# Attention and feed-forward outputs through DRAM as one float32 array, split where they are loaded

## The chip, the cores and the metric

The kernel runs on one core of one Trainium2 chip. The metric is the device time of one execution in microseconds (us); the median of three runs of the kernel before is 1112.55 us. A core has five engines with a queue of instructions each: PE (TensorE, matrix products), DVE (VectorE), ACT (ScalarE), POOL (GpSimd) and SP (SyncE, which issues every DMA of this kernel).

## The reference

Causal attention with a forget gate over 4 batches x 8 heads of 576 positions and 64 dimensions, then two feed-forward layers of 512 to 2048 to 512 on the 2304 tokens:

```
scores = q @ k.T / sqrt(64) + cum[:, None] - cum[None, :]   # cum: running sum of log f; causal mask
attn   = softmax(scores);  x = (attn @ v) laid out as [2304, 512]
h = maximum(x @ w_in, 0);  y = (h * h) @ w_out              # first layer
h = y @ w_in2;  out = (h - tanh(h)) @ w_out2                # second layer
```

## The kernel before

Products in float32 are made from PE's reduced form of it, called fp32r here: an operand is split into a high part, which is its rounding to fp32r (`rounded()`, a copy on ACT, POOL or DVE, L89, L91, L93), and a rest, the operand less that (`rest()`, a subtraction, L102). A product is then the sum of three: high x high, low x high, high x low.

The heads are numbered u = 0 to 31, eight per batch. The feed-forward work goes in blocks: j = 0 to 7 are the first layer on 288 tokens each (two blocks per batch), j = 8 to 12 the second layer on 512 (the last on 256). A block has 16 steps, one per chunk i of 128 of the 2048 hidden units. An h step (`h_step`, L140) is 12 matmuls into the one PSUM bank `hp` (there are three banks from block 6 on), followed by the nonlinearity on ACT and the split into `gh` and `gl` (first layer) or `ghl` (second). A y step (`y_step`, L166) is 12 matmuls into four banks `yp`; it comes two h steps later.

Attention is cut into pieces that are advanced between these steps, a certain number per step (`PACE`, `advance`), so that PE has feed-forward work while a head waits for the other engines. All heads of a batch have to be stored before the blocks of that batch can load their X. Up to block 2 each engine's order is fixed from a first build; from there on the order is set by the framework's scheduler, which runs a model of the engines over the program. So the order of all engines may move when an instruction is taken out.

The heads from 16 on take another way for the transposition of the softmax's P: DVE transposes 32x32 blocks into `T` (L471 to L477), `put` writes `T` to DRAM (`p_d<-T`, 1 MB), `get` reads it in four pieces (`PTl<-p_d`, 1 MB), `split_p` splits it on POOL (`PTh`, L91) and DVE (`PTl`, L102), and `pv` makes `o_ps` on PE (L517 to L522), then `xt` on ACT and `xs` on DVE.

The outputs that go through DRAM are kept there already split:

- `store_x` (L404) takes two finished heads in `xs` and makes the high part `xsh` (ACT for u from 16, POOL below) and the rest in place (POOL), and stores the two with one DMA each (L410, L411) in `x_d`. The first 320 tokens of batch 0 are handled in `first`, with small pieces `XE`.
- `y_out` (L667) does the same with the four `yp` banks of a block: ACT rounds, DVE subtracts (both read PSUM), and two DMAs store the two parts `yst` in `y_d` (L683).
- `load_x` (L700) reads high and low part of a block's X: two DMAs in the first layer (L707, asked for at i = 13 of the block before), four in the second (L714, at i = 4; for block 8 at i = 13 of block 7).

X of the first layer, `yst`, and `ghl` come from one pool tag `xhl` of four buffers.

The weights are fetched raw, in float64 (`raw`, L111), and split on ACT (L121, `w` L89), DVE (L122 to L124) and POOL or DVE (`w` L102). The second layer's first six chunks are split during blocks 6 and 7 (`w2_early`), the other ten at the end of block 7 (`w2_late`).

Of the kernel before, what the change touches and what calls it, by code (L numbers as in the profile page):

```python
# [21 lines left out]
NF = DFF // 128  # L22
# [25 lines left out]
TB = 288  # L48
TB2 = 512
# [5 lines left out]
def kernel(  # L55
# [10 lines left out]
    nc = tc.nc  # L66

    misc = ctx.enter_context(tc.tile_pool(name="misc", bufs=1))
    wpool = ctx.enter_context(tc.tile_pool(name="w", bufs=1))
    psy = ctx.enter_context(tc.tile_pool(name="psy", bufs=1, space=bass.MemoryType.PSUM))  # L70
    dram = ctx.enter_context(tc.tile_pool(name="dram", bufs=1, space=bass.MemoryType.DRAM))

    aug_d = dram.tile([NU, 4, 2, S], F32, name="aug_d")
    x_d = [dram.tile([NK, 128, 2, S], F32, name=f"x_d{b}") for b in range(B)]
    p_d = [dram.tile([128, 2048], F32, name=f"p_d{a}") for a in range(2)]
    y_d = dram.tile([NK, 128, 2, NTOK], F32, name="y_d")

    ident = misc.tile([128, 128], F32, name="ident")
    mk = misc.tile([128, S], F32, name="mk")
# [1 line left out]
    def pre(u):  # L81
        return "" if u < UT else "l_"

    def by(name):
        return {"A": nc.scalar, "V": nc.vector, "P": nc.gpsimd, "S": nc.sync}[ENG[name]]

    def rounded(eng, out, in_):
        if eng is nc.scalar:
            eng.activation(out, in_, AF.Copy)  # L89
        elif eng is nc.gpsimd:  # L90
            eng.tensor_scalar(out, in_, 1.0, 1.0, ALU.mult, ALU.mult)  # L91
        else:
            eng.tensor_copy(out, in_)  # L93
# [7 lines left out]
    def rest(eng, out, in_, hi):  # L101
        eng.tensor_tensor(out, in_, hi.bitcast(F32), ALU.subtract)  # L102
# [160 lines left out]
    def bank0(part, name):  # L263
        if part:
            return psa.tile([128, 512], F32, tag="at", name=name)
        pool, tag = ROT[rot[0] % len(ROT)]
        rot[0] += 1
        return pool.tile([128, 512], F32, tag=tag, name=name)

    def first(h, part):  # L270
# [15 lines left out]
        p = {}  # L286
# [51 lines left out]
        def o_step():  # L338
            ps = bank0(part, "o_ps")
            t0 = tiles[0]  # L340
            for c in ((0, 2, 3, 4, 1) if part else (0, 2, 1)):
                if c == 4:
                    nc.tensor.matmul(ps[0:64, 128:256], vr[0:64, 4], ptr[0][:, 0:128], start=False, stop=False)
                    continue
                t = max(t0, c)
                nc.tensor.matmul(ps[0:64, (t - t0) * 128:256], vr[:, c], pt[0][:, c, t - 1:t0 + 1].rearrange("p t j -> p (t j)"),
                                 start=(c == 0), stop=(c == 1))
            if not part:
                ps0 = bank0(part, "o0_ps")
                nc.tensor.matmul(ps0[0:64, 0:64], vr[0:64, 0], ptr[0][:, 0:64], start=True, stop=True)  # L350
            e = h % 2
            if e == 0:
                XS[0] = two.tile([128, S], F32, tag="xs", name="xs")
            xs = XS[0]
            rr = slice(64 * e, 64 * e + 64)
            c0 = 320 if part else 64
            rounded(by("b_xs" if part else "a_xs"), xs[rr, c0:c0 + 256], ps[0:64, 0:256])
            if not part:
                rounded(by("a_xs0"), xs[rr, 0:64], ps0[0:64, 0:64])
            if e == 1:  # L360
                if part:
                    store_x(0, h // 2, xs, 320, S)
                else:
                    rounded(nc.scalar, X[0][0][:, h // 2], xs[:, :TB])
                    rest(by("a_xl"), X[0][1][:, h // 2], xs[:, :TB], X[0][0][:, h // 2])
                    rounded(nc.scalar, XE[:, 0, h // 2].bitcast(F32R), xs[:, TB:320])
                    rest(nc.gpsimd, XE[:, 1, h // 2], xs[:, TB:320], XE[:, 0, h // 2])
                    if h == H - 1:
                        for a in range(2):
                            nc.sync.dma_start(x_d[0][:, :, a, TB:320].rearrange("k p n -> p k n"), XE[:, a])  # L370

        return s_step, t_step, o_step

    def first_a(also):
        st = {}
        for h in range(H + 3):
            if h < H:
                st[h] = first(h, 0)
                for t in (2, 1, 0):
                    st[h][0](t)  # L380
            if h >= 2 and h - 2 < H:
                for t in (2, 1, 0):
                    st[h - 2][1](t)
            if h >= 3:
                st[h - 3][2]()
            also(h)
# [16 lines left out]

    def store_x(b, pair, xs, c0, c1):  # L404
        STORED.add((b, pair, c1))
        n = c1 - c0
        xh = one.tile([128, S], F32R, tag="xsh", name="xsh")
        rounded(by(pre(b * H) + "xh"), xh[:, :n], xs[:, c0:c1])
        rest(by(pre(b * H) + "xl"), xs[:, c0:c1], xs[:, c0:c1], xh[:, :n])
        nc.sync.dma_start(x_d[b][pair][:, 0, c0:c1], xh[:, :n].bitcast(F32))  # L410
        nc.sync.dma_start(x_d[b][pair][:, 1, c0:c1], xs[:, c0:c1])  # L411

    def row_min(p, ps, st, t, i, a, b, mn):
        n = NKEY[t]
# [80 lines left out]
    def pv(u):  # L495
# [42 lines left out]
        if e == 1:  # L538
            store_x(b, h // 2, xs, 0, S)
# [126 lines left out]

    def y_out(tok, last):  # L667
        if last:
            y2 = [[wpool.tile([128, 2, TB], F32R, tag=f"w{NF - 2 + a}_{r}", name="yst") for r in range(2)] for a in range(2)]
        else:  # L670
            y2 = [f1.tile([128, NK, TB], F32R, tag="xhl", bufs=4, name="yst") for _ in range(2)]

        def emit(m, ps):
            yh, yl = (y[m // 2][:, m % 2] if last else y[:, m] for y in y2)
            rounded(nc.scalar, yh, ps)
            rest(by("yl"), yl, ps, yh)
            if last and m % 2:
                for a in range(2):
                    dst = y_d[m - 1:m + 1, :, a, tok:tok + TB].rearrange("k p n -> p k n")
                    nc.sync.dma_start(dst, y2[a][m // 2].bitcast(F32))  # L680
            elif not last and m == NK - 1:
                for a in range(2):
                    nc.sync.dma_start(y_d[:, :, a, tok:tok + TB].rearrange("k p n -> p k n"), y2[a].bitcast(F32))  # L683
        return emit

    def out_emit(j, tok, n):
# [10 lines left out]
    NB = NTOK // TB  # L697
    BLK = [(1, j * TB, TB) for j in range(NB)] + [(2, t, min(TB2, NTOK - t)) for t in range(0, NTOK, TB2)]

    def load_x(j):  # L700
        ph, tok, n = BLK[j]
        if ph == 1:
            b, c = divmod(tok, S)
            assert all((b, m, S) in STORED for m in range(NK))
            xs = [f1.tile([128, NK, TB], F32R, tag="xhl", bufs=4, name="xhl") for _ in range(2)]
            for a, x in enumerate(xs):
                nc.sync.dma_start(x.bitcast(F32), x_d[b][:, :, a, c:c + n].rearrange("k p n -> p k n"))  # L707
            return xs
        xs = [[wpool.tile([128, 2, TB2], F32R, tag=f"w{NF - 6 + 2 * a + r}_{(j - NB) % 2}", name="xhl")[:, :, :n]
               for r in range(2)] for a in range(2)]  # L710
        for a in range(2):
            for r in range(2):
                src = y_d[2 * r:2 * r + 2, :, a, tok:tok + n].rearrange("k p n -> p k n")
                nc.sync.dma_start(xs[a][r].bitcast(F32), src)  # L714
        return xs

    late = None

# [18 lines left out]
    for g in range(len(BLK) * NF + LAG):  # L737
        j, i = divmod(g, NF)
        if (j, i) == MARK:
            first_part = {x.name for x in nc.cur_bb.bb.instructions}  # L740
        if j < len(BLK):
            ph, _, n = BLK[j]
# [21 lines left out]
        if jy >= 0:  # L764
            ph, tok, n = BLK[jy]
            if iy == 0:
                Y[jy] = [psy.tile([128, 512], F32, tag=f"y{m}", name="yp") for m in range(NK)]
            y_step(ph, iy, G.pop(g - LAG), Y[jy], n)
            if jy >= NB - 1:
                w2_late((jy - NB + 1) * NF + iy, 1)  # L770
            if iy == NF - 1:
                emit = y_out(tok, jy == NB - 1) if ph == 1 else out_emit(jy, tok, n)
                for m in range(NK):
                    emit(m, Y[jy][m][:, :n])
                X.pop(jy)
# [6 lines left out]
    last = {}  # L782
# [56 lines left out]
```

## Time and profile before

| | us |
|---|---|
| three runs, median (lowest, highest) | 1112.55 (1110.88, 1115.29) |
| the profiled execution | 1113.58 |
| its span | 1111.7 |
| PE busy in it | 1036.8 |
| DVE busy | 647.3 |
| ACT busy | 525.7 |
| POOL busy | 297.5 |

The execution is 1.9 us longer than the span that the profiler sees. Shares of busy time are means over stretches that differ: up to 60 us a prologue; to 296 the heads below 16 beside the first blocks; to 565 the late heads; to 708 the rest of the first layer and the weights of the second; then the second layer. Line numbers such as L102 are those of the kernel before.

### The profile page before, as it was taken

Reading aid. Unit: us, or ns where it says so; the run is one execution under the profiler, and the core shown is the slowest. Engines: PE = TensorE matmul, PEld = TensorE weight load, DVE = VectorE, ACT = ScalarE, POOL = GpSimd, SP = SyncE. Lnnn points to the kernel's source line nnn. Section 1 sums busy time; section 2 is a strip of 40 time slices with the busy share of each in tenths; the row PEclk is TensorE's granted clock in tenths of the full one; section 3 lists DMA queues with packets and bytes.
Section 4 is the critical chain, followed back from the end, with each engine's and each line's share of the span. In section 5 each row is a group of like instructions: output and inputs, shape, how many; then the busy total and the mean of one; then the engine's idle time right before and its main releaser. Section 6 shows DMA issues by size and latency. Waiting matters only on the chain.

```text
span 1111.7 us, 17017 instructions
## 1 busy us (share of the span) xinstructions
PE 1036.8 (93%) x6048; PEld 903.0 (81%) x6048; DVE 647.3 (58%) x1631; ACT 525.7 (47%) x1221; POOL 297.5 (27%) x389
## 2 busy tenths in 40 slices
PE   3989989999999798999897997999999999999998
PEld 2577668888998787988797997888888888888898
DVE  7799987777787777787549169722222222222222
ACT  5777777665556455465346466522222222222222
POOL 4144555564453443443224024200000000000000
PEclk9999999999999999999998999999999999999999
DMA  6556643225955648755473086300300200110010
GB/s 198 217 146 187 174 159 120 79 85 176 288 174 177 191 166 251 227 166 174 134 253 124 1 292 224 100 1 1 114 1 1 80 35 1 38 38 1 1 39 20
DMA packets 63302, 134.84 MB, mean 121 GB/s; under 512 B 6416, under 2 KB 31568, under 8 KB 61168
## 3 DMA queue, kind: packets, MB, share of 16 engines
q1 hardware_dynamic: 63216, 133.74, 38.0%
q8 instruction: 48, 0.79, 0.3%
q14 instruction: 38, 0.31, 0.1%
HBM read 93.94 MB, written 39.78 MB: 120 GB/s over the span
## 4 chain that ended last, share of the span: by engine, by line
PE 52%; DMA 10%; DVE 6%; issue 3%; POOL 2%; SPq 1%; ACT 1%; POOLq 0%; ACTq 0%; DVEq 0%
PE yp L166 25%; PE hp L140 24%; DMA PTl<-p_d 6%; DMA p_d<-T 3%; PE o_ps L520 2%; DVE PTl L102 2%; DMA raw<-in_w_dram 1%; SPq L486 1%; DVE gl L102 1%; DVE wst L122 1%; DVE wst L123 1%; POOL PTh L91 1%; DVE wst L124 1%; PE s_ps L444 0%; DVE T L474 0%
## 5 line engine op out<-in xcount | busy, mean ns | idle before, releaser
L140 PE MATMUL hp<-xhl,w 128*128 128x288 f32 (+2 forms) x2496 | 455.0, 330 | 2.3 <-ACT tmp L150 0.9
L140 PEld LDWEIGHTS hp<-xhl,w 128*128 128x128 f32 x2496 | 389.9, 192 | 39.5 <-ACT tmp L150 1.9
L166 PE MATMUL yp<-ghl,w 128*128 128x512 f32 (+1 forms) x960 | 216.0, 374 | 0.0
L166 PE MATMUL yp<-gh,w 128*128 128x288 f32 x1024 | 199.3, 300 | 1.8 <-ACT gh L151 1.8
L166 PEld LDWEIGHTS yp<-ghl,w 128*128 128x128 f32 x960 | 168.4, 188 | 34.5
L155 DVE TENSOR_TENSOR tmp<-hp,tmp 128x512 f32<-128x512 f32 (+1 forms) x80 | 51.0, 637 | 228.6 <-ACT tmp L154 228.6
L166 PEld LDWEIGHTS yp<-gh,w 128*128 128x128 f32 x1024 | 161.6, 192 | 4.1 <-ACT gh L151 2.0
L154 ACT ACTIVATE tmp<-hp 128x512 f32<-128x512 f32 (+1 forms) x80 | 44.4, 555 | 243.0 <-PE hp L140 243.0
L166 PE MATMUL yp<-gl,w 128*128 128x288 f32 x512 | 134.4, 303 | 17.2 <-DVE gl L102 16.6
L166 PEld LDWEIGHTS yp<-gl,w 128*128 128x128 f32 x512 | 90.5, 191 | 21.9 <-DVE gl L102 20.0
L150 ACT ACTIVATE tmp<-hp 128x288 f32<-128x288 f32 x128 | 51.9, 406 | 115.0 <-PE hp L140 111.1
L427 ACT ACTIVATE P<-P,ST 128x320 f32<-128x320 f32 (+4 forms) x151 | 84.5, 561 | 35.9 <-DVE ST L418 34.7
L431 POOL TENSOR_SCALAR P<-P,ST 128x448 f32<-128x448 f32 (+4 forms) x88 | 59.7, 681 | 102.5 <-DVE ST L430 59.7
L102 DVE TENSOR_TENSOR gl<-tmp,gh 128x288 fp32r<-128x288 f32 x96 | 58.2, 606 | 46.9 <-ACT tmp L152 46.7
L102 DVE TENSOR_TENSOR ghl<-tmp,ghl 128x512 fp32r<-128x512 f32 (+1 forms) x80 | 51.1, 638 | 49.2 <-ACT ghl L89 49.2
L418 DVE CUSTOM_DVE_ANT_0 P<-s_ps,mk 128x320 f32<-128x320 f32 (+3 forms) x151 | 63.5, 431 | 18.5 <-PE s_ps L445 12.5
L102 DVE TENSOR_TENSOR PTl<-PTl,PTh 128x512 fp32r<-128x512 f32 (+1 forms) x64 | 51.9, 840 | 36.8 <-POOL PTh L91 36.7
L102 POOL TENSOR_TENSOR w<-wst,w 128x512 fp32r<-128x512 f32 x32 | 46.7, 1468 | 98.8 <-ACT w L89 96.8
L89 ACT ACTIVATE ghl<-tmp 128x512 fp32r<-128x512 f32 (+1 forms) x80 | 47.2, 590 | 53.6 <-DVE tmp L155 53.5
L91 POOL TENSOR_SCALAR PTh<-PTl 128x512 fp32r<-128x512 f32 (+1 forms) x64 | 46.4, 752 | 57.7 <-DMA PTl<-p_d 56.7
L124 DVE SCALAR_TENSOR_TENSOR wst<-wst 128x512 uint32<-128x512 uint32 x64 | 57.4, 898 | 1.0
L151 ACT ACTIVATE gh<-tmp 128x288 fp32r<-128x288 f32 x128 | 56.6, 443 | 2.9
(122 smaller groups left out, 1294.5 us busy)
## 6 DMA issues: line engine op xcount, KB each, us to landing
raw<-in_w_dram SPq DMA_DIRECT2D x64, 512.0 KB
p_d<-T SPq DMA_DIRECT2D x16, 1024.0 KB
PTl<-p_d SPq DMA_DIRECT2D x64, 256.0 KB
R<-in_qk_dram SPq DMA_DIRECT2D x24, 576.0 KB
xhl<-y_d SPq DMA_DIRECT2D x16, 512.0 KB
xhl<-x_d SPq DMA_DIRECT2D x14, 576.0 KB
y_d<-yst SPq DMA_DIRECT2D x14, 576.0 KB
VR<-in_v_dram SPq DMA_DIRECT2D x32, 160.0 KB
```

What stands on the lines that cost most here:

```text
L89: eng.activation(out, in_, AF.Copy)
L91: eng.tensor_scalar(out, in_, 1.0, 1.0, ALU.mult, ALU.mult)
L102: eng.tensor_tensor(out, in_, hi.bitcast(F32), ALU.subtract)
L124: nc.vector.scalar_tensor_tensor(tu, x.bitcast(U32), 3, tu, ALU.logical_shift_left, ALU.bitwise_or)
L140: nc.tensor.matmul(ps, w[:, k * 128:(k + 1) * 128], xk, start=(jj == 0), stop=(jj == 11))
L150: nc.scalar.activation(tmp, ps, AF.Relu)
L151: nc.scalar.activation(gh, tmp, AF.Square)
L155: nc.vector.tensor_tensor(tmp, ps, tmp, ALU.subtract)
L166: nc.tensor.matmul(yp[m][:, :n], w[:, c], x, start=(i == 0 and j == 0), stop=(i == NF - 1 and j == 2))
L418: nc.vector.tensor_tensor_reduce(p[:rows, a:b], ps[:rows, :b - a], mk[:rows, o:o + b - a], -0.125, 3.0e38 if mn is None else mn, ALU.add, ...
L427: nc.scalar.activation(p[:rows, :n], p[:rows, :n], AF.Exp, bias=mn, scale=-1.0, accum_out=st[:rows, 1, t:t + 1])
L431: by(n_by).tensor_scalar(p[:rows, :n], p[:rows, :n], st[:rows, 3, t:t + 1], 1.0, ALU.mult, ALU.mult)
```

## The change

`x_d` and `y_d` hold one float32 array each. `store_x` is one DMA from `xs`, and its rounding and rest are gone; the first part stores its 32 last columns straight from `xs`, with one DMA per pair of heads. `y_out` is one copy on ACT per bank and one DMA. `load_x` reads the plain array into the buffer of the low part, then ACT rounds it into the buffer of the high part, and the rest is taken in place, by POOL in the first layer and by DVE in the second; both in two halves. `y_out` takes one buffer of the tag `xhl` rather than two.

```
     aug_d = dram.tile([NU, 4, 2, S], F32, name="aug_d")
-    x_d = [dram.tile([NK, 128, 2, S], F32, name=f"x_d{b}") for b in range(B)]
+    x_d = [dram.tile([NK, 128, S], F32, name=f"x_d{b}") for b in range(B)]
...
-    y_d = dram.tile([NK, 128, 2, NTOK], F32, name="y_d")
+    y_d = dram.tile([NK, 128, NTOK], F32, name="y_d")
...
-                    rounded(nc.scalar, XE[:, 0, h // 2].bitcast(F32R), xs[:, TB:320])
-                    rest(nc.gpsimd, XE[:, 1, h // 2], xs[:, TB:320], XE[:, 0, h // 2])
-                    if h == H - 1:
-                        for a in range(2):
-                            nc.sync.dma_start(x_d[0][:, :, a, TB:320].rearrange("k p n -> p k n"), XE[:, a])
+                    nc.sync.dma_start(x_d[0][h // 2][:, TB:320], xs[:, TB:320])
...
     def store_x(b, pair, xs, c0, c1):
         STORED.add((b, pair, c1))
-        n = c1 - c0
-        xh = one.tile([128, S], F32R, tag="xsh", name="xsh")
-        rounded(by(pre(b * H) + "xh"), xh[:, :n], xs[:, c0:c1])
-        rest(by(pre(b * H) + "xl"), xs[:, c0:c1], xs[:, c0:c1], xh[:, :n])
-        nc.sync.dma_start(x_d[b][pair][:, 0, c0:c1], xh[:, :n].bitcast(F32))
-        nc.sync.dma_start(x_d[b][pair][:, 1, c0:c1], xs[:, c0:c1])
+        nc.sync.dma_start(x_d[b][pair][:, c0:c1], xs[:, c0:c1])
...
         if last:
...
         else:
-            y2 = [f1.tile([128, NK, TB], F32R, tag="xhl", bufs=4, name="yst") for _ in range(2)]
+            y = f1.tile([128, NK, TB], F32, tag="xhl", bufs=4, name="yst")
 
         def emit(m, ps):
-            yh, yl = (y[m // 2][:, m % 2] if last else y[:, m] for y in y2)
-            rounded(nc.scalar, yh, ps)
-            rest(by("yl"), yl, ps, yh)
+            nc.scalar.activation(y[m // 2][:, m % 2] if last else y[:, m], ps, AF.Copy)
...
             elif not last and m == NK - 1:
-                for a in range(2):
-                    nc.sync.dma_start(y_d[:, :, a, tok:tok + TB].rearrange("k p n -> p k n"), y2[a].bitcast(F32))
+                nc.sync.dma_start(y_d[:, :, tok:tok + TB].rearrange("k p n -> p k n"), y)
...
-            xs = [f1.tile([128, NK, TB], F32R, tag="xhl", bufs=4, name="xhl") for _ in range(2)]
-            for a, x in enumerate(xs):
-                nc.sync.dma_start(x.bitcast(F32), x_d[b][:, :, a, c:c + n].rearrange("k p n -> p k n"))
-            return xs
...
+            xl, xh = (f1.tile([128, NK, TB], F32R, tag="xhl", bufs=4, name="xhl") for _ in range(2))
+            nc.sync.dma_start(xl.bitcast(F32), x_d[b][:, :, c:c + n].rearrange("k p n -> p k n"))
             for r in range(2):
...
+                k = slice(2 * r, 2 * r + 2)
+                rounded(nc.scalar, xh[:, k], xl[:, k].bitcast(F32))
+                rest(by("xl"), xl[:, k], xl[:, k].bitcast(F32), xh[:, k])
+            return xh, xl
...
+        for r in range(2):
+            nc.sync.dma_start(xl[r].bitcast(F32), y_d[2 * r:2 * r + 2, :, tok:tok + n].rearrange("k p n -> p k n"))
+            rounded(nc.scalar, xh[r], xl[r].bitcast(F32))
+            rest(nc.vector, xl[r], xl[r].bitcast(F32), xh[r])
+        return xh, xl
```

The order moves at two places that matter. The first is PE's queue at the last late head (u = 31), in block 5. The number at the end of a weight tile's name counts the tiles of the build; before, `w_0_1350` is chunk 9 of the block and `w_0_1248` chunk 8.

```order
L140 MATMUL hp<-xhl,w_0_1248 128x288 x12
L166 MATMUL yp<-gh,w_1_1158 128x288 x8
L166 MATMUL yp<-gl,w_1_1158 128x288 x4
L520 MATMUL o_ps<-PTh,VH 128x512
L522 MATMUL o_ps<-PTl,VR 64x64
L140 MATMUL hp<-xhl,w_0_1350 128x288 x12
L520 MATMUL o_ps<-PTh,VH 128x512
L166 MATMUL yp<-gh,w_1_1256 128x288 x8
L520 MATMUL o_ps<-PTl,VH 128x512
```

Now the same stands around chunk 6 (`w_0_1043`; `w_0_949` is chunk 5, and the lines of `pv` are L511 and L513).

```order
L140 MATMUL hp<-xhl,w_0_949 128x288 x12
L166 MATMUL yp<-gh,w_1_868 128x288 x8
L166 MATMUL yp<-gl,w_1_868 128x288 x4
L511 MATMUL o_ps<-PTh,VH 128x512
L513 MATMUL o_ps<-PTl,VR 64x64
L140 MATMUL hp<-xhl,w_0_1043 128x288 x12
L511 MATMUL o_ps<-PTh,VH 128x512
L166 MATMUL yp<-gh,w_1_957 128x288 x8
L511 MATMUL o_ps<-PTl,VH 128x512
```

The last head's product has moved forward by three steps of h and y, which now follow it.

The second place is DVE's queue at the end of block 7, where the second layer begins: L122 to L124 split weights, `gl` belongs to the first layer, L155 to the second. Before:

```order
L122 TENSOR_SCALAR wst<-raw 128x512
L124 SCALAR_TENSOR_TENSOR wst<-wst 128x512
L123 SCALAR_TENSOR_TENSOR wst<-raw,wst 128x512
L122 TENSOR_SCALAR wst<-raw 128x512
L102 TENSOR_TENSOR gl<-tmp,gh 128x288
L124 SCALAR_TENSOR_TENSOR wst<-wst 128x512
L123 SCALAR_TENSOR_TENSOR wst<-raw,wst 128x512
L124 SCALAR_TENSOR_TENSOR wst<-wst 128x512
L102 TENSOR_TENSOR gl<-tmp,gh 128x288
L155 TENSOR_TENSOR tmp<-hp,tmp 128x512
L102 TENSOR_TENSOR ghl<-tmp,ghl 128x512
```

Now:

```order
L102 TENSOR_TENSOR xhl<-xhl 128x1024
L123 SCALAR_TENSOR_TENSOR wst<-raw,wst 128x512
L102 TENSOR_TENSOR gl<-tmp,gh 128x288
L122 TENSOR_SCALAR wst<-raw 128x512
L124 SCALAR_TENSOR_TENSOR wst<-wst 128x512
L123 SCALAR_TENSOR_TENSOR wst<-raw,wst 128x512
L102 TENSOR_TENSOR xhl<-xhl 128x1024
L124 SCALAR_TENSOR_TENSOR wst<-wst 128x512
L102 TENSOR_TENSOR gl<-tmp,gh 128x288 x2
L102 TENSOR_TENSOR xhl<-xhl 128x1024
L155 TENSOR_TENSOR tmp<-hp,tmp 128x512
L102 TENSOR_TENSOR ghl<-tmp,ghl 128x512
```

Three of four rests of the loaded X (the fourth stands six rows further ahead) have come in among the last weights and the last `gl`s of the first layer.

## Rows read from the trace of the kernel before

**Rows 1.** The page: span, and busy time, share and instructions of each engine.
```profile
span 1111.7 us, 17017 instructions
...
PE 1036.8 (93%) x6048; PEld 903.0 (81%) x6048; DVE 647.3 (58%) x1631; ACT 525.7 (47%) x1221; POOL 297.5 (27%) x389
```

**Rows 2.** Busy time by stretch: length, PE, PEld, DVE, ACT, POOL, clock, DMA share, GB/s.
```profile
60.00:296.00 236.00, 222.77 (x1409) 188.06 (x1409) 201.53 (x573) 165.36 (x395) 121.81 (x164) 0.99 0.51 155
296.00:420.00 124.00, 113.78 (x763) 105.94 (x763) 93.17 (x286) 66.35 (x170) 54.79 (x69) 0.97 0.59 184
420.00:565.00 145.00, 134.47 (x898) 125.56 (x897) 98.00 (x284) 72.22 (x187) 54.14 (x71) 0.96 0.60 180
...
656.00:708.00 52.00, 43.35 (x287) 40.69 (x286) 49.70 (x65) 33.58 (x70) 25.52 (x18) 0.97 0.68 230
708.00:1112.00 404.00, 399.69 (x1913) 332.30 (x1911) 109.03 (x175) 97.51 (x173) 1.28 (x1) 1.00 0.08 28
```

**Rows 3.** Waits of PE, 296 to 565: waited for; total us, times, longest.
```profile
PE o_ps L520 <- POOL PTh L91: 16.4, 9, 4.1
```

**Rows 4.** The chain of waits, 296 to 565: start, duration, what.
```profile
302.59 0.58 ACT xsh L89
...
303.24 1.45 POOL xs L102
304.71 0.34 SPq L411
...
316.05 4.13 DMA p_d<-T
...
321.55 6.06 DMA PTl<-p_d
...
398.56 5.05 DMA PTl<-p_d
...
413.78 3.88 DMA p_d<-T
...
419.06 6.65 DMA PTl<-p_d
...
530.13 6.70 DMA PTl<-p_d
```

**Rows 5.** Timeline of PE at 563: start, duration, instruction.
```profile
563.20 1.76 PE L140 MATMUL hp<-xhl,w 128*128 128x288 f32 x12
...
566.39 1.76 PE L140 MATMUL hp<-xhl,w 128*128 128x288 f32 x12
```

**Rows 6.** Waits of PE, 565 to 708.
```profile
PE yp L166 <- DVE gl L102: 13.8, 9, 4.0
```

**Rows 7.** Tile `gl` on DVE, 656 to 708: durations min/median/max in ns; who waited.
```profile
L102 DVE TENSOR_TENSOR gl<-tmp,gh x11: 443/456/1554, 660.9 to 706.6; 128x288 fp32r<-128x288 f32 x11
...
  PE yp L166: 8.6, 7
```

**Rows 8.** Groups by line and form: busy us, mean ns of one, idle before it.
```profile
L102 DVE TENSOR_TENSOR ghl<-tmp,ghl 128x512 fp32r<-128x512 f32 x64 | 44.3, 692 | 41.9 <-ACT ghl L89 41.9
...
L102 POOL TENSOR_TENSOR xs<-xs,xsh 128x576 f32<-128x576 f32 x12 | 17.5, 1457 | 14.5 <-ACT xsh L89 14.2
...
L102 DVE TENSOR_TENSOR yst<-yp,yst 128x288 fp32r<-128x288 f32 x32 | 13.2, 440 | 0.0
...
L89 ACT ACTIVATE xsh<-xs 128x576 fp32r<-128x576 f32 x8 | 5.4, 679 | 4.8 <-DVE xs L532 4.8
```

**Rows 9.** Timeline of SP (SPq: time in which it issues) at 647.
```profile
647.40 0.99 SPq L683 DMA_DIRECT2D y_d<-yst  x1
```

**Rows 10.** Timeline of DVE at 657, with its idle time before in brackets.
```profile
656.84 0.76 DVE L122 TENSOR_SCALAR wst<-raw 128x512 uint32<-128x512 uint32 x2 [1.97 <-DMA raw<-in_w_dram]
```

**Rows 11.** Tile `yst` on DVE, whole span.
```profile
L102 DVE TENSOR_TENSOR yst<-yp,yst x32: 409/443/458, 185.1 to 712.3; 128x288 fp32r<-128x288 f32 x32
```

**Rows 12.** The page: DMA issues.
```profile
y_d<-yst SPq DMA_DIRECT2D x14, 576.0 KB
```

More of the change, by code (lines that the diff above doesn't have):

```diff
@@ L631 @@
     TA = one.tile([128, 2048], F32, tag="T", name="TA")
-    XE = TA[:, 1024:1280].rearrange("p (a k n) -> p a k n", a=2, k=NK)
     first_a(weights_early)
@@ L668, in y_out @@
         if last:
-            y2 = [[wpool.tile([128, 2, TB], F32R, tag=f"w{NF - 2 + a}_{r}", name="yst") for r in range(2)] for a in range(2)]
+            y = [wpool.tile([128, 2, TB], F32, tag=f"w{NF - 2}_{r}", name="yst") for r in range(2)]
         else:
-            y2 = [f1.tile([128, NK, TB], F32R, tag="xhl", bufs=4, name="yst") for _ in range(2)]
+            y = f1.tile([128, NK, TB], F32, tag="xhl", bufs=4, name="yst")
         def emit(m, ps):
-            yh, yl = (y[m // 2][:, m % 2] if last else y[:, m] for y in y2)
-            rounded(nc.scalar, yh, ps)
-            rest(by("yl"), yl, ps, yh)
+            nc.scalar.activation(y[m // 2][:, m % 2] if last else y[:, m], ps, AF.Copy)
             if last and m % 2:
-                for a in range(2):
-                    dst = y_d[m - 1:m + 1, :, a, tok:tok + TB].rearrange("k p n -> p k n")
-                    nc.sync.dma_start(dst, y2[a][m // 2].bitcast(F32))
+                nc.sync.dma_start(y_d[m - 1:m + 1, :, tok:tok + TB].rearrange("k p n -> p k n"), y[m // 2])
             elif not last and m == NK - 1:
-                for a in range(2):
-                    nc.sync.dma_start(y_d[:, :, a, tok:tok + TB].rearrange("k p n -> p k n"), y2[a].bitcast(F32))
+                nc.sync.dma_start(y_d[:, :, tok:tok + TB].rearrange("k p n -> p k n"), y)
         return emit
@@ L704, in load_x @@
             assert all((b, m, S) in STORED for m in range(NK))
-            xs = [f1.tile([128, NK, TB], F32R, tag="xhl", bufs=4, name="xhl") for _ in range(2)]
-            for a, x in enumerate(xs):
-                nc.sync.dma_start(x.bitcast(F32), x_d[b][:, :, a, c:c + n].rearrange("k p n -> p k n"))
-            return xs
-        xs = [[wpool.tile([128, 2, TB2], F32R, tag=f"w{NF - 6 + 2 * a + r}_{(j - NB) % 2}", name="xhl")[:, :, :n]
-               for r in range(2)] for a in range(2)]
-        for a in range(2):
-            for r in range(2):
-                src = y_d[2 * r:2 * r + 2, :, a, tok:tok + n].rearrange("k p n -> p k n")
-                nc.sync.dma_start(xs[a][r].bitcast(F32), src)
-        return xs
+            xl, xh = (f1.tile([128, NK, TB], F32R, tag="xhl", bufs=4, name="xhl") for _ in range(2))
+            nc.sync.dma_start(xl.bitcast(F32), x_d[b][:, :, c:c + n].rearrange("k p n -> p k n"))
+            for r in range(2):
+                k = slice(2 * r, 2 * r + 2)
+                rounded(nc.scalar, xh[:, k], xl[:, k].bitcast(F32))
+                rest(by("xl"), xl[:, k], xl[:, k].bitcast(F32), xh[:, k])
+            return xh, xl
+        xl, xh = ([wpool.tile([128, 2, TB2], F32R, tag=f"w{NF - 6 + 2 * a + r}_{(j - NB) % 2}", name="xhl")[:, :, :n]
+                   for r in range(2)] for a in range(2))
+        for r in range(2):
[3 more added lines that the diff above has]
+        return xh, xl
     late = None
```

## The prediction

> **What bounds the kernel now.** I read the page's busy shares first, then the busy time by stretch, then the waits of PE in the stretches that are not full, then the chain there. PE is busy 93% of a span of 1111.7 us [rows 1], so only what changes PE's idle time, some 75 us, can change the end. The table by stretch tells where that idle time lies [rows 2]: 708 to 1112 has 399.69 busy of 404, so nothing done there by another engine matters unless it grows a lot. The late attention, 296 to 565, leaves 10.2 and 10.5 us, at granted clocks of 0.97 and 0.96. The end of the first feed-forward layer, 656 to 708, leaves 8.65 of 52, and there DVE is busy 49.70. These two places have two different owners.
>
> In the late attention PE waits for `PTh`, made by POOL: 16.4 us in nine waits of up to 4.1 [rows 3]. POOL itself waits for a transfer: the chain of waits goes, per head, from the transposes into `T`, through a 1 MB write `p_d<-T` of some 4 us and a 1 MB read `PTl<-p_d` of 5 to 6.7, to the splitting of P [rows 4]. There are sixteen such heads. Between them PE works on feed-forward steps, the filler. One step of h and y is 3.2 us, from 563.20 to 566.39 [rows 5].
>
> In 565 to 708 PE waits 13.8 us for `gl` (DVE) in nine waits [rows 6], 8.6 us of it in seven waits from 656 on [rows 7], where DVE splits the weights of the second layer and has 2.3 us of idle left.
>
> **The change part by part.** The sum is made on the profiled execution, 1111.7 of span and 1.9 around it, 1113.6; the median of the three runs is 1112.55, so 1.0 goes off at the end.
>
> *Prologue and first layer up to 296 us.* Eight small roundings and rests of 128x32 and the second DMA of each go; the raw weights that SP issues behind the new x stores are not needed until long after. Two splits of 128x576 per block come in on ACT and POOL. ACT's wait in its queue for the load, and behind them stand the Relus that free the one `hp` bank. The load is asked for two to three steps ahead (i = 13 of 16), 6 to 10 us, against a landing for which the nearest row is a 1 MB read of 5 to 6.7 [rows 4]; a load of half of that should come sooner. PE is at 222.77 of 236 here [rows 2]. I take 0, with −3 if the six lost roundings help (each 0.68 on ACT or 1.46 on POOL [rows 8]) and +3 if ACT stands in its queue for about a us in three blocks.
>
> *Late attention.* Three things come off the chain: at 302.59 it runs through the rounding `xsh` (0.58) and the rest `xs` (1.45) to the store's issue on SP at 304.71, and only behind that SP issues the fourth piece of the read [rows 4]. One plain store remains, so 2.1 us go, once (in the other heads the reads are issued before or long after). Two reads, at 419.06 and 530.13, took 6.65 and 6.70 where 6.0 to 6.1 is usual, both behind an x store; with the store halved I give three heads 0.5 each, 1.5. Against that stands what the order of PE shows: the scheduler thinks that the heads have become quicker and puts the last head's `o_ps` around chunk 6 of block 5, where they stood around chunk 9; three steps of h and y now lie behind the attention. As filler they are lost: 3 x 3.2 = 9.6 us more of waiting if the round trip of a head stays as it is. Nine heads wait today; the other seven have up to some 2 us to spare, and since the lost filler is 0.6 per head, they absorb part of it. Of 7 x 0.6 = 4.2 I count 3.0. Sum: 9.6 − 2.1 − 1.5 − 3.0 = +3.0. Ends: +9.6 when nothing of the rest helps, −11.2 when each round trip is shorter too (first rival).
>
> *After the attention, 565 to 656.* The early weights of the second layer now arrive with three steps of block 5 still to do, and their twelve splits stand within five `gl`s rather than six, but the four `yst` rests between them go (0.44 each [rows 8], 1.8). The store of y is one DMA of 576 KB [rows 12] rather than two. I take −1 (−4 to +3): PE's waits on `gl` here are 13.8 − 8.6 = 5.2 us, which bounds the gain.
>
> *Transition, 656 to 708.* The order of DVE shows four rests of 128x1024 of the second layer's first X between the last `gl`s and the last weights; before, nothing of the kind stood there. No row shows this shape. A rest of 128x288 takes 0.440 and one of 128x512 0.692 [rows 8]; by the slope, (0.692 − 0.440)/224 per column, 1024 columns give 0.692 + 512 x 0.00113 = 1.27, so four give 5.1. PE waits for DVE at nearly every step there, so nearly all of it counts; as a part of it will fall into the 2.3 us in which DVE is idle, I take +4.5. What goes: block 6's second y store. SP issued it at 647.40 for 0.99 us, between the raw weights [rows 9], and 0.59 MB [rows 12] less goes ahead of them; at the 230 GB/s of this stretch [rows 2] that is 2.6 us, and DVE stood 1.97 us waiting for raw weights at 656.84 [rows 10]. I take −2.2, between the two. Together +2.3, from −2 (the rests fall into what DVE still waits) to +7.
>
> Here a shared port may bite. Every `yst` rest (one operand in PSUM) took 409 to 458 ns, all 32 of them [rows 11]. The `gl` rests, both operands in SBUF, took 443 to 1554 ns in 656 to 708, where POOL makes `w` rests [rows 7]: up to 1.1 us more for one. The Trainium skill, page "SBUF — State Buffer", section "Who interferes with whom", has it that a DVE instruction with two SBUF inputs contends with a GpSimd one that reads SBUF, and that one of the two is blocked outright; the trace agrees, at 1554 against 443 ns. The removed rests were of the immune kind, and the added ones have both operands in SBUF.
>
> *Second layer, 708 to the end.* The other four loads have six more rests on DVE and as many roundings on ACT; DVE is busy 109 of 404 and ACT 97.5 [rows 2]. 0.
>
> Sum: 0 + 3.0 − 1 + 2.3 + 0 = +4.3, 1117.9, and on the scale of the median 1116.8.
>
> **The rivals.**
> First, faster: the round trip gets shorter. x and y traffic halves, and all transfers go by one queue. The fastest write and read in the chain took 3.88 and 5.05, against 4.13 and 6.06 at the head of 316 [rows 4]: 1.3 us less in sixteen heads is 20.8. With the 9.6 of filler gone that leaves −11.2, and with the other terms (−1 + 2.3) 1113.6 − 9.9 − 1.0 = 1103. For it: 16.4 us of `PTh` waits and clocks below 1.00 there, both of which would go. Against it: what leaves the late attention is a few MB beside 16 x 2 MB of P, and some trips with no x store near them took 6 us as well. Chance 0.28.
>
> Second, slower: the lost filler becomes wait in full. The place is `o_ps` behind `PTh`; the price 9.6 us, with nothing absorbed and nothing off the chain, because the 2.1 is seen once and the head that it helps then waits for the next write. It decides as soon as the read of a head lands later than its place among PE's steps for most of the sixteen heads rather than nine. 1113.6 + 9.6 − 1 + 2.3 − 1.0 = 1123.5. For it: the order is fixed, and a queue that comes too early simply stands. Chance 0.26.
>
> Third, slower by the port: the four new rests at the transition are blocked by POOL as the `gl` rests are, 1.1 each on top, 4.4: 1113.6 + 4.3 + 4.4 − 1.0 = 1121.3. For it the `gl` rows [rows 7]; against it that only some of the rests meet a POOL operation. This is the page's rule, with its price from the rows. Chance 0.08.
>
> That the bytes don't halve is excluded: one array stands where there were two.
>
> **How the numbers follow.** The forecast, the sum, has 0.38; its own range is 1111 to 1121. What a measurement can tell from no change is 0.5%, 5.6 us, so faster is below 1107.0 and slower above 1118.1. The first rival is faster, 0.28. The second and third are slower, 0.34, and of the forecast's own range a small part lies above 1118.1 and a part of the second's and third's cases below it, which I let cancel but for 0.01: slower 0.35, same 0.37. The range takes in the first rival and the second with half of its spread: 1102 to 1128.
>
> **What would show it.** Late attention: the wait of `o_ps` on `PTh` from 16.4 to some 19 to 20 (forecast), under 10 (first rival), about 26 (second), with the write and read of a head at 4.1 and 6.1, or at 3.9 and 5.1. Transition: a DVE rest of 128x1024 at about 1.3 four times before the first `tmp<-hp` of 512 columns, or 2.4 (third rival), and PE's waits on `gl` there at 11 instead of 8.6. Second layer: PE idle no more than 4 to 5 us of 404. I am wrong in the mechanism if the first 296 us move by over 3 us, which would mean ACT's place in its queue behind the loads counts, or if `p_d` trips change with no change in what PE waits for.

## The result, and the profile after

The changed kernel takes 1124.39 us (median of four runs, 1122.91 to 1131.92) against 1113.92 of the kernel before (four runs beside it, 1110.88 to 1119.15): ratio 1.010, 95% interval 1.0068 to 1.0132, slower. The time lies in the range, at the second rival's 1123.5, 7.6 over the forecast's 1116.8 and outside the forecast's own 1111 to 1121. The profiled execution took 1125.66 us, its span is 1123.9.

The page after, with PE's busy time and DVE's up by 5 us and ACT's by 13 [rows 1]:

```profile
span 1123.9 us, 16930 instructions
...
PE 1041.5 (93%) x6048; PEld 905.6 (81%) x6048; DVE 652.0 (58%) x1609; ACT 538.8 (48%) x1233; POOL 294.4 (26%) x375
```

Busy time by stretch after, columns as in [rows 2]; the transition is cut 656 to 720, as it ends later:

```profile
60.00:296.00 236.00, 222.20 (x1386) 186.07 (x1385) 197.52 (x565) 164.86 (x393) 115.71 (x153) 0.99 0.46 137
296.00:420.00 124.00, 112.31 (x755) 104.65 (x754) 90.55 (x280) 66.40 (x170) 46.53 (x63) 0.97 0.56 164
420.00:565.00 145.00, 129.16 (x842) 119.12 (x841) 94.36 (x270) 68.72 (x175) 56.50 (x70) 0.95 0.52 154
...
656.00:720.00 64.00, 54.26 (x358) 51.49 (x357) 59.09 (x76) 42.91 (x86) 28.64 (x20) 0.95 0.57 191
720.00:1123.00 403.00, 399.86 (x1914) 332.45 (x1912) 113.94 (x177) 102.81 (x179) 1.40 (x1) 1.00 0.06 20
```

From 296 to 565 PE was busy for 241.47 us where it was for 248.25 before [rows 2], so it stood 6.8 us longer, with less DMA (0.56 and 0.52 of the engines, 0.59 and 0.60 before). PE's waits in that stretch, columns as in [rows 3]:

```profile
PE o_ps L511 <- POOL PTh L91: 19.5, 12, 4.4
PE hp L140 <- ACT tmp L150: 2.9, 3, 1.3
PE yp L166 <- DVE gl L102: 2.1, 2, 1.7
PE o_ps L511 <- DVE ST L409: 1.2, 1, 1.2
```

The wait on `PTh` is 19.5 where 16.4 stood, what the forecast said (19 to 20). The wait on `tmp`, ACT's first operation on an h step, took 0.4 us in all before:

```profile
PE hp L140 <- ACT tmp L150: 0.4, 1, 0.4
```

A read of P still takes some 6 us; in the chain of waits from 296 to 560, columns as in [rows 4]:

```profile
320.89 5.99 DMA PTl<-p_d
...
338.43 6.03 DMA PTl<-p_d
...
355.85 5.25 DMA PTl<-p_d
...
373.11 3.84 DMA p_d<-T
...
378.31 6.63 DMA PTl<-p_d
...
526.78 6.88 DMA PTl<-p_d
```

The most useful view was one that I worked out: the first matmul of a block's first h step, found by counting PE's `hp` matmuls in twelves and 16 steps to a block. Block 2 is where the late heads begin, block 6 the first without attention, block 8 the second layer. "Ahead" is the count of h steps started before the last late head's last product with `VH`. Starts and lengths are in us, each from one execution. How far they repeat can be seen twice: e8, e10 and the changed kernel have PE's order in common up to 706 us, and take 310.9 to 312.8 over blocks 2 to 5; the kernel before, e2, e4 and e6 have the same prologue, and start block 0 at 54.7 to 59.2.

| kernel (profiled execution) | block 0 starts | block 2 starts | blocks 2 to 5 | blocks 6, 7 | ahead | ratio to before (95%) |
|---|---|---|---|---|---|---|
| before | 56.5 | 280.4 | 295.6 | 125.6 | 90 | 1 |
| changed | 51.2 | 274.2 | 312.8 | 126.2 | 87 | 1.010 (1.0068, 1.0132) |
| e1 new code, old PE order | 50.0 | 272.3 | 324.9 | 131.6 | 90 | 1.0209 (1.0182, 1.0236) |
| e2 old code, new PE order | 54.7 | 277.8 | 321.6 | 124.2 | 87 | 1.0184 (1.0157, 1.0212) |
| e3 x only | 50.9 | 273.9 | 306.1 | 130.7 | 89 | 1.0044 (1.0022, 1.0066) |
| e4 y only | 59.2 | 281.5 | 295.9 | 128.8 | 89 | 1.0011 (0.9994, 1.0028) |
| e5 new code, later heads | 51.0 | 272.7 | 309.8 | 126.3 | 91 | 1.0073 (1.0047, 1.0099) |
| e6 old code, earlier heads | 57.1 | 281.0 | 302.6 | 128.7 | 88 | 1.0069 (1.0049, 1.0089) |
| e7 dummy XE operations | 58.2 | 279.9 | 311.6 | 126.0 | 87 | 1.012 (1.0099, 1.0141) |
| e8 rests on POOL | 51.3 | 272.7 | 312.5 | 128.5 | 87 | 1.0118 (1.0096, 1.014) |
| e9 stores made twice | 52.8 | 277.7 | 309.0 | 126.4 | 90 | 1.0071 (1.0046, 1.0096) |
| e10 no rests at the transition | 51.4 | 272.8 | 310.9 | 126.1 | 87 | 1.0119 (1.0091, 1.0146) |
| e11 old code, plain tail | 55.3 | 280.4 | 294.1 | 127.3 | 90 | 0.9979 (0.9957, 1.0) |
| e12 no X splits in layer 1 | 52.7 | 274.7 | 296.6 | 129.1 | 88 | 0.9951 (0.9929, 0.9972) |

So the change gains 6.2 us up to block 2, loses 17.2 in blocks 2 to 5, 0.6 in blocks 6 and 7 and 0.5 behind them: 12.1 between these two executions, 10.5 by the medians.

Not all of the 17.2 is waiting. Blocks 2 to 5 as one stretch, before and after, columns as in [rows 2]:

```profile
280.40:576.00 295.60, 274.84 (x1855) 257.69 (x1854) 207.60 (x619) 153.00 (x391) 115.90 (x148) 0.97 0.64 193
```

```profile
274.20:587.00 312.80, 280.37 (x1843) 259.13 (x1842) 222.71 (x622) 160.41 (x404) 128.60 (x157) 0.96 0.57 172
```

PE stands 11.7 us longer (32.4 against 20.8), and is busy 5.5 us longer for twelve instructions fewer, at a granted clock of 0.96 instead of 0.97.

### The profile page after: what moved, and what is told of

Same layout as the page of the kernel before. It is cut to its first block, busy times and chain, and to the rows that moved or that the text cites. A ratio compares the mean times of both kernels' runs of the same rounds, so it can differ in the third digit from the quotient of the medians.

```text
span 1123.9 us, 16930 instructions
## 1 busy us (share of the span) xinstructions
PE 1041.5 (93%) x6048; PEld 905.6 (81%) x6048; DVE 652.0 (58%) x1609; ACT 538.8 (48%) x1233; POOL 294.4 (26%) x375
## 4 chain that ended last, share of the span: by engine, by line
PE 64%; DVE 15%; DMA 12%; issue 5%; SPq 2%; POOL 2%; ACT 1%; POOLq 0%; ACTq 0%; DVEq 0%
PE yp L166 27%; PE hp L140 26%; DMA PTl<-p_d 8%; PE o_ps L511 3%; DVE wst L123 2%; DVE wst L124 2%; DMA p_d<-T 2%; DVE wst L122 2%; SPq L477 1%; DVE PTl L102 1%; PE s_ps L435 1%; PE o_ps L346 1%; DVE QA L102 1%; DVE w L102 1%; DMA raw<-in_w_dram 1%
## 5 line engine op out<-in xcount | busy, mean ns | idle before, releaser
L155 DVE TENSOR_TENSOR tmp<-hp,tmp 128x512 f32<-128x512 f32 (+1 forms) x80 | 51.0, 638 | 220.1 <-ACT tmp L154 220.1
L166 PE MATMUL yp<-gl,w 128*128 128x288 f32 x512 | 131.9, 304 | 19.9 <-DVE gl L102 19.0
L418 ACT ACTIVATE P<-P,ST 128x320 f32<-128x320 f32 (+4 forms) x151 | 84.7, 562 | 52.6 <-DVE ST L409 50.9
L422 POOL TENSOR_SCALAR P<-P,ST 128x448 f32<-128x448 f32 (+4 forms) x88 | 63.2, 720 | 112.6 <-DVE ST L421 49.2
L102 DVE TENSOR_TENSOR PTl<-PTl,PTh 128x512 fp32r<-128x512 f32 (+1 forms) x64 | 51.4, 839 | 41.9 <-POOL PTh L91 41.8
L89 ACT ACTIVATE ghl<-tmp 128x512 fp32r<-128x512 f32 (+1 forms) x80 | 47.1, 589 | 55.3 <-DVE tmp L155 55.2
L409 DVE CUSTOM_DVE_ANT_0 P<-s_ps,mk 128x320 f32<-128x320 f32 (+3 forms) x151 | 63.3, 432 | 17.2 <-PE s_ps L436 15.1
L89 ACT ACTIVATE w<-wst 128x512 fp32r<-128x512 f32 x64 | 40.3, 630 | 38.1 <-DVE wst L124 37.8
```

The costliest lines, as they stand in the source:

```text
L155: nc.vector.tensor_tensor(tmp, ps, tmp, ALU.subtract)
L166: nc.tensor.matmul(yp[m][:, :n], w[:, c], x, start=(i == 0 and j == 0), stop=(i == NF - 1 and j == 2))
L409: nc.vector.tensor_tensor_reduce(p[:rows, a:b], ps[:rows, :b - a], mk[:rows, o:o + b - a], -0.125, 3.0e38 if mn is None else mn, ALU.add, ...
L418: nc.scalar.activation(p[:rows, :n], p[:rows, :n], AF.Exp, bias=mn, scale=-1.0, accum_out=st[:rows, 1, t:t + 1])
L422: by(n_by).tensor_scalar(p[:rows, :n], p[:rows, :n], st[:rows, 3, t:t + 1], 1.0, ALU.mult, ALU.mult)
```

## The experiments

The changed kernel's parts can be had alone, so the first question was which part loses, and the second whether it is PE's order. Each kernel was timed in five rounds beside the kernel before.

**One part alone.** e3 keeps `y_out`, `y_d` and the second layer's loads of the kernel before; e4 keeps `store_x`, `first` and the first layer's loads. The edits are the change's own, taken by halves.

> Only x travels as one array; y keeps its two. The scheduler now puts 89 h steps ahead of the last late head, one step fewer than before. Theory A: 5 us gained by the prologue, 3.2 us lost by one step, nothing added at the transition to the second layer: 1109 to 1115 us. Theory B: the splits of x on ACT and POOL are the ones beside the attention, so 1118 to 1123 us.

> Only y travels as one array; x keeps its two. Again 89 h steps ahead of the last late head. Theory A: 3.2 us for the one step, 2.6 us for the four rests of 128x1024 on DVE at the transition: 1117 to 1121 us. Theory B: no split of x is added, so only the transition costs: 1114 to 1118 us.

Measured: x only 1121.37 us, y only 1117.48. x alone gains the prologue and loses 10.5 us in blocks 2 to 5; y alone neither (0.3). For x theory B's range held and theory A's did not; y lies in both. The loss starts with x, but x alone has 10.5 of the 17.2 us; the other 6.7 come only with both halves together, though y alone costs nothing there.

**PE's order.** e1 and e2 hold PE's instructions from block 2 on in the other kernel's order, as a list of runs of program positions (the cut shows the loop that does it, without the list):

```
+    for a, n in json.loads(zlib.decompress(base64.b85decode(PE_ORDER))):
+        for x in pe[a:a + n]:
...
+            if prev is not None:
+                tc.add_manual_dep(x, prev, same_order, reason="order")
+            prev = x.name
```

> The changed kernel, with PE's queue from block 2 on held in the order of the kernel before (90 h steps ahead of the last late head's last product, not 87). Theory A, the order costs it: the lost filler was 3 steps of 3.2 us, 9.6 us, so this takes 1112 to 1116 us, and the waits of PE on PTh in the late attention fall from 19.5 us to about 15 or less. Theory B, the new splits on ACT and POOL slow the heads themselves, whatever the order: 1121 to 1125 us.

> The kernel before, with PE's queue from block 2 on held in the order of the changed kernel (87 h steps ahead of the last late head's last product instead of 90). Theory A: 1113.9 + 9.6, 1121 to 1125 us, with the last late head at the same time as before and three more steps behind it. Theory B: within 3 us of the kernel before, 1111 to 1117 us.

Measured: 1139.62 and 1136.78 us. Both are far slower than either kernel, with the 90 steps as with the 87, and both lose it in blocks 2 to 5. Neither theory had that. PE's order in their traces is the other kernel's, but ACT's, DVE's and POOL's are then neither kernel's, which the scheduler ordered anew. So these two runs compare more than PE's order; why both lose was not found, and they settle nothing on the change. The order was then moved by its own knob and the scheduler left to keep the engines in step (`CUT` says how many pieces of attention stand ahead of a block):

```
e5, changed kernel:             e6, kernel before:
-CUT = (25, 44, 61, 2)          -CUT = (25, 44, 61, 2)
+CUT = (24, 43, 60, 2)          +CUT = (27, 46, 62, 2)
```

> The changed kernel with one piece of attention fewer ahead of each of three blocks (CUT 24, 43, 60 instead of 25, 44, 61), so that the scheduler itself, with all engines in step, puts 91 h steps ahead of the last late head instead of 87. Theory A', steps lost as filler become waits: four steps of 3.2 us come back, 1110 to 1115 us, with the last late head not later than in the changed kernel by more than 3 us. Theory C, the loop of a head (read of P, split, product, next read) is filled either way and a head given more filler just ends later: 1120 to 1126 us, the last head some 10 us later.

> The kernel before with two pieces more ahead of blocks 3 and 4 and one ahead of 5 (CUT 27, 46, 62), so that the scheduler puts 88 h steps ahead of the last late head instead of 90. Theory A': two steps of 3.2 us lost, 1118 to 1123 us. Theory C: no change, 1112 to 1117 us.

Measured: e5 1123.21, e6 1122.44 us. In the old code two steps of filler fewer cost 0.69%, 7.7 us, as theory A' said and a little more. The price of two steps, 6.4 us, agrees with that; the place does not: the wait on `PTh` is 16.8 where it was 16.4, and PE's waits in e6 from 296 to 565 are spread over more releasers than before:

```profile
PE o_ps L520 <- POOL PTh L91: 16.8, 10, 3.5
PE o_ps L520 <- DVE ST L429: 2.8, 4, 1.3
PE hp L140 <- ACT tmp L150: 1.9, 3, 1.0
PE yp L166 <- DVE gl L102: 1.8, 4, 0.6
```

In the new code four steps more gave back 3 us in blocks 2 to 5, and 3 by the ratio, not 12.8: the last late head's last product with `VH` starts at 567.7 instead of 557.9, so theory C holds there. The last try at the order puts the lost transfers back, without their computation, by which the scheduler goes back to 90 steps by itself:

```
         nc.sync.dma_start(x_d[b][pair][:, c0:c1], xs[:, c0:c1])
+        nc.sync.dma_start(x_e[b][pair][:, c0:c1], xs[:, c0:c1])
...
+                nc.sync.dma_start(y_e[:, :, tok:tok + TB].rearrange("k p n -> p k n"), y)
```

> The changed kernel, with each store of x and y after the first part issued a second time into an array that nothing reads: the transfers and SP issues that the change took away come back, with no computation. The scheduler, all engines in step, then puts 90 h steps ahead of the last late head's last product again (87 in the changed kernel), and at the heads from 20 on nearly where the kernel before has them. Theory D, the loss in the late attention is that order, which the scheduler chose because its model of the transfers got shorter and the chip's head did not: 1111 to 1118 us, faster than the changed kernel in spite of the extra traffic. Theory C, a head ends later by what filler it is given: 1122 to 1128 us.

Measured: 1122.51 us, in theory C's range of 1122 to 1128 (single executions took 1115.01 to 1129.9; the profiled one, 1127.24, is among the longer). More traffic cost nothing, but the time did not return to 1114: by the ratio theory D explains some 3 us of the 10. What the fourteen kernels say of the count "ahead" is that it does not order them: 88 steps stand in e6 and in e12, whose ratios are 1.0069 and 0.9951, 13 us apart.

**The splits of X.** e12 takes the splits of the loaded X of the first layer out of the changed kernel:

```
             nc.sync.dma_start(xl.bitcast(F32), x_d[b][:, :, c:c + n].rearrange("k p n -> p k n"))
-            for r in range(2):
-                k = slice(2 * r, 2 * r + 2)
-                rounded(nc.scalar, xh[:, k], xl[:, k].bitcast(F32))
-                rest(by("xl"), xl[:, k], xl[:, k].bitcast(F32), xh[:, k])
-            return xh, xl
+            return xl, xl
```

> The changed kernel without the splits of the loaded X of the first layer: blocks 1 to 7 use the loaded tile as high and low part (their result is not the reference's), so that the 14 roundings on ACT and 14 rests on POOL, and one buffer per block, are gone. The scheduler puts 88 h steps ahead of the last late head. If these splits beside the late heads are what costs beyond the order: 3.2 us for one step and 4 to 6 more come back, 1113 to 1118 us. If they hide: 1120 to 1125 us, the changed kernel less at most one step.

Measured: 1109.67 us, under the range given and under the kernel before. Blocks 2 to 5 take 296.6 us, 16.2 less than in the changed kernel, at one step more ahead; PE is busy for 245.84 us from 296 to 565 instead of 241.47. This is the only edit that gave the loss back, and it gave back nearly all of it: the fourteen roundings and fourteen rests, with the buffer, the order and the waits that come with them, are what the change costs. PE's wait on `PTh` from 296 to 565 goes from 19.5 us to 15.5, and of the 16.2 us PE stands for 8.9 less and is busy for 7.3 less, at a granted clock of 0.98. The wait, and then blocks 2 to 5 in e12:

```profile
PE o_ps L511 <- POOL PTh L91: 15.5, 9, 3.5
```

```profile
274.70:571.30 296.60, 273.04 (x1846) 255.09 (x1844) 206.97 (x616) 152.27 (x386) 112.21 (x145) 0.98 0.60 180
```

The table says the same of the other kernels. Leaving out e1 and e2, the seven that split the loaded X take 306.1 to 312.8 us over blocks 2 to 5, whatever else was changed in them; the five that don't split it there take 294.1 to 302.6, and the highest of these is e6, whose heads were put earlier.

A part of how they do it can be read at the start of block 2. ACT in the changed kernel (start, duration, instruction; in brackets its idle time before and what ended it):

```profile
273.12 1.26 ACT L89 ACTIVATE xhl<-xhl 128x576 fp32r<-128x576 f32 x2 [3.13 <-DMA xhl<-x_d]
274.28 1.29 ACT L664 ACTIVATE yst<-yp 128x288 f32<-128x288 f32 x4
...
280.73 0.41 ACT L150 ACTIVATE tmp<-hp 128x288 f32<-128x288 f32 x1
```

SP there, and POOL:

```profile
265.25 0.38 SPq L691 DMA_DIRECT2D xhl<-x_d  x1
```

```profile
275.13 3.27 POOL L102 TENSOR_TENSOR xhl<-xhl 128x576 fp32r<-128x576 f32 x2
```

The load is issued at 265.25; ACT stands 3.13 us until it has landed, nearly 8 us after the issue; the rests end at 278.40. The block's first h step, whose last four matmuls need the low part, is taken to pieces in PE's queue:

```profile
274.23 0.43 PE L140 MATMUL hp<-xhl,w 128*128 128x288 f32 x2
...
276.02 0.96 PE L140 MATMUL hp<-xhl,w 128*128 128x288 f32 x6
...
278.59 0.43 PE L140 MATMUL hp<-xhl,w 128*128 128x288 f32 x2
...
279.15 0.43 PE L140 MATMUL hp<-xhl,w 128*128 128x288 f32 x2
...
281.19 1.87 PE L140 MATMUL hp<-xhl,w 128*128 128x288 f32 x12 [0.70 <-ACT tmp L150]
...
285.33 1.86 PE L140 MATMUL hp<-xhl,w 128*128 128x288 f32 x12
```

Between the pieces PE does the attention's matmuls. With one `hp` bank the second step cannot start before the first has been read: 7.0 us from the first to the second. In e12 the same steps:

```profile
274.73 1.76 PE L140 MATMUL hp<-xhl,w 128*128 128x288 f32 x12
...
278.81 1.76 PE L140 MATMUL hp<-xhl,w 128*128 128x288 f32 x12
...
282.66 1.85 PE L140 MATMUL hp<-xhl,w 128*128 128x288 f32 x12
```

4.1 us, whole. The changed kernel has three more pairs of `s_ps` products between these two steps, which e12 makes before its third step; counted to the third step it is 11.1 us against 7.9. The same wait of ACT comes again before block 4's X, in ACT's queue ahead of the `tmp` of an h step that is done; PE does not wait for that `tmp`:

```profile
422.70 1.26 ACT L89 ACTIVATE xhl<-xhl 128x576 fp32r<-128x576 f32 x2 [2.95 <-DMA xhl<-x_d]
423.86 0.39 ACT L150 ACTIVATE tmp<-hp 128x288 f32<-128x288 f32 x1
```

Over the span it is 7.4 us in three waits; the view of tile `xhl` on ACT, what its engine waited for:

```profile
  DMA xhl<-x_d: 7.4, 3
```

These are the even blocks, 2, 4 and 6, whose batch has only just been stored. At blocks 2 and 4 the store is not all that holds the load: SP issues it right behind the four reads of a head's P, 5.2 and 5.6 us after the last store of x; at block 4:

```profile
410.21 0.33 SPq L402 DMA_DIRECT2D x_d<-xs  x1
413.93 1.74 SPq L477 DMA_DIRECT2D PTl<-p_d  x4
415.77 0.38 SPq L691 DMA_DIRECT2D xhl<-x_d  x1
```

At block 6, with no such reads between, it is 2.1 us. Whether an earlier place in SP's queue would help was not run.

About 3 us at block 2 are visible in this way, and they are not the whole account. In e9, which splits the same X, the second step of block 2 follows 4.5 us after the first, and blocks 2 to 5 still take 309.0. Nor does ACT's stand order the losses: it is 10.6 us in e3, which loses 10.5, and 7.4 in the changed kernel, which loses 17.2. How the other 13 divide between such waits, the new work on ACT (14 x 0.68 us) and POOL (14 x 1.44) among the heads' own operations, the buffer, the clock and the order that the scheduler makes of it, no run tells apart: none moved the splits to another engine, or left them out and kept the buffer and the order.

**The prologue.** e7 puts the eight small operations back into the changed kernel; e11 takes them out of the kernel before.

```
e7:  +                    rounded(nc.scalar, XE[:, 0, h // 2].bitcast(F32R), xs[:, TB:320])
     +                    rest(nc.gpsimd, XE[:, 1, h // 2], xs[:, TB:320], XE[:, 0, h // 2])
e11: +                    nc.sync.dma_start(t_d[h // 2], xs[:, TB:320])
     +            if e:
     +                nc.sync.dma_start(xs[1].bitcast(F32)[:, :, :e], t_d.rearrange("k p n -> p k n"))
     +                rounded(nc.scalar, xs[0][:, :, :e], xs[1][:, :, :e].bitcast(F32))
     +                rest(by("xl"), xs[1][:, :, :e], xs[1][:, :, :e].bitcast(F32), xs[0][:, :, :e])
```

(Starts of h steps are counted in these expectations from the trace's first record, 11 us ahead of the span's zero; 11 goes off for the table's.)

> The changed kernel with the eight small roundings and rests of 128x32 of the first part put back (their results are not used; x is still stored plain), to see whether these are what brought the first h step from 67.5 forward to 62.5 in the profile. If they are: the first h step of block 0 at 66 to 68 us again and 1126 to 1130 us. If the earlier start has another cause, or varies from build to build: first h step at 61 to 64, 1122 to 1127 us.

> The kernel before with only the first part's 32 last columns changed: they go to DRAM plain from xs (the eight 128x32 operations of the prologue are gone) and are split, by two operations of 128x128, when block 1 loads its X; all else, and the place of every late head among the h steps (90 ahead of the last), is as before. If the 5 us that the changed kernel gains in the prologue last as long as the late attention is left alone: first h step near 62, 1108 to 1111 us, faster than before. If the late attention swallows the lead whatever the code: 1112 to 1116 us.

Measured: e7 1127.94 us, and its first h step starts at 58.15, not 51.2, which is later than expected (55 to 57 on the table's scale). The eight kernels of the new prologue without the operations start at 50.0 to 52.8, so that the operations held it up is shown for the new code. e11 took 1112.9 us, in its second range, 0.2% under the kernel before, with its first h step at 55.3 and block 2 at the same 280.4 as before. So in the old code nearly nothing of the lead came, for a reason that no run shows, and whether the late attention keeps a lead was not tested by it; e12, which starts block 2 at 274.7 and ends faster than before, says that it can. Of the kernels that leave nothing out e11 is the fastest, by 0.2%, at the edge of what five rounds tell. The version that the runs point to next, x split where it is stored and the prologue of the changed kernel, was not run.

**The transition.** e8 moves the second layer's rests from DVE to POOL (`rest(nc.gpsimd, ...)`); e10 leaves out those of blocks 8 and 9 (`if j > NB + 1:` ahead of the `rest`).

> The changed kernel with the rests of the second layer's X on POOL, which is idle after 720 us, instead of DVE. If the four DVE rests of 128x1024 (1.21 us each) are what the transition lost: 2 to 5 us less than the changed kernel, 1119 to 1122 us, and the stretch from block 7's sixth h step to block 8's second back from 53.6 to about 50 us. If POOL's longer rests hold up its weight rests and with them DVE: no gain or a loss, 1123 to 1128 us.

> The changed kernel without the four DVE rests of 128x1024 at the transition: blocks 8 and 9 use the loaded X itself as low part (their result is not the reference's). If these rests are what the transition lost: 4 x 1.2 = 4.8 us at most, 1119 to 1122 us, and PE's waits on gl from 656 to 722 down from 9.7 to about 5 us. If DVE there waits for the weights or POOL anyway: 1123 to 1126 us, waits 9 us or more.

Measured: 1127.38 and 1127.42 us, the second above both of its ranges. Neither gains; the stretch that the first expectation puts at 53.6 us took 55.6 in e8 and 55.5 in e10. PE's waits from 656 to 720 in the changed kernel, and then in e10:

```profile
PE yp L166 <- DVE gl L102: 9.7, 7, 2.3
```

```profile
PE yp L166 <- DVE gl L102: 11.7, 8, 3.4
```

Without 4.8 us of DVE work PE waits no less. e3, which has no such rests either, takes longer over blocks 6 and 7 than the changed kernel (130.7 and 126.2 us).

## Why the prediction was right and wrong

The range held, and the sign of what I called likeliest did not: no change was forecast, with 0.35 for slower. That the time lies in the range is luck in part: a gain of 6 us in the prologue and a loss of 17 in blocks 2 to 5, against 0 and +3.0 in the sum, are two errors of opposite signs.

*The step that failed* is the one that put the two splits of 128x576 per block at 0, −3 to +3, under "Prologue and first layer up to 296 us", and then not at all in the late attention. I had counted the load's lead of "two to three steps" at i = 13 and ACT's stand at "about a us in three blocks"; it was 7.4 us in three. What the runs show in its place is that these splits, with what comes with them, cost 16 us of blocks 2 to 5 (e12), not 0. One piece of it can be named: the path at the start of an even block is store, load, round, rest, h step in a row, where it was store, load, h step, and with one `hp` bank a late low part stops the h steps behind it, which are the filler of the heads. That is some 3 us at block 2; the cause of the rest stays open.

*The prologue* was put at 0, −3 to +3, and gained 5.3 us at the first h step and 6.2 by block 2. That is over the 3 us that I had named as the sign of a wrong mechanism, but it went the other way, and not by ACT's place behind the loads. The operations of 128x32 were small in themselves, 0.2 to 0.3 us each and one of 0.7; I did not follow what stands behind them in ACT's and POOL's queues.

*Late attention.* "Nine heads wait": there are twelve waits now, 19.5 us, as forecast, but that is 3.1 us of a loss of 17.2, so the sign came true without the mechanism. The read of P takes 6 us as it did, so the first rival (3.88 and 5.05) is out; the reads behind an x store, given 0.5 less each, still took 6.63 and 6.88. Two lost steps cost what their price says in the old code (e6: 7.7 us), though not as a wait on `PTh`. That the three lost steps are the main term is wrong: giving them back returned some 3 us (e5, e9). The time was that of the second rival, but its wait of 26 us did not come; its mechanism is a part of it at best.

*Transition.* The rest of 128x1024 was put at 1.27 us and takes 1.215 (median below). PE's waits on `gl` there are 9.7 us, where 11 was the forecast's sign. That four of the rests cost +4.5 there is not borne out (e10, e3): blocks 6 and 7 together moved by +0.6 where this term and the one ahead of it summed to +1.3. The third rival priced a stretch of these rests by POOL; the view of tile `xhl` on DVE (durations min/median/max) shows none:

```profile
L102 DVE TENSOR_TENSOR xhl<-xhl x10: 693/1215/1228, 706.0 to 980.7; 128x1024 fp32r<-128x1024 f32 x8, 128x512 fp32r<-128x512 f32 x2
```

It was POOL that paid. Two rests started on DVE just before a weight rest on POOL, and that one took 2.15 and 2.28 us where the one ahead of them took 1.54 and those before it 1.4; DVE's timeline, then POOL's:

```profile
715.44 1.22 DVE L102 TENSOR_TENSOR xhl<-xhl 128x1024 fp32r<-128x1024 f32 x1
...
719.02 1.21 DVE L102 TENSOR_TENSOR xhl<-xhl 128x1024 fp32r<-128x1024 f32 x1
```

```profile
711.52 1.54 POOL L102 TENSOR_TENSOR w<-wst,w 128x512 fp32r<-128x512 f32 x1 [1.63 <-ACT w L89]
715.66 2.15 POOL L102 TENSOR_TENSOR w<-wst,w 128x512 fp32r<-128x512 f32 x1 [2.60 <-ACT w L89]
719.11 2.28 POOL L102 TENSOR_TENSOR w<-wst,w 128x512 fp32r<-128x512 f32 x1 [1.30 <-ACT w L89]
```

The Trainium skill, page "SBUF — State Buffer", section "Who interferes with whom", says that the order of issue decides which of the two blocks; these rows agree, at 0.75 and 0.9 us over the usual 1.4.

*Second layer.* 0 was right: PE 399.86 busy of 403.

## What to carry to other kernels

An operation that moves from the store's side to the load's side changes place on the path: it now stands between the last store and the first use, in the queue of an engine that serves others. Price the latency that it adds there and what waits behind it in that queue, beside its busy time and the bytes that it saves; take the operation out for one run and see what comes back before tuning anything round it. Look at PE's busy time as well as at its waits: here PE was busy, not waiting, for 5.5 of the 17.2 us lost. And when PE's queue is fixed in another kernel's order, see whether the other engines' orders stayed; here they did not, so move it by a knob of the program and read what moved.

## What was not expected of the hardware

Of the hardware, only which engine the shared port holds up (0.75 and 0.9 us on POOL, none on DVE's rests of 128x1024, above). Of the program: some 6 us gained in the changed kernel's prologue by leaving out eight operations of 0.2 to 0.7 us each, where the kernel before gained 1 us by the same, and two kernels 1.8 and 2.1% slower from another order of PE's instructions and what the scheduler made of it.
